# Three edits at the seam between attention and expert layers: hits in halves, two products on VectorE, a part of layer 1 moved

## The chip, the cores and the metric

The kernel runs on one core of a Trainium2 chip. The metric is the device time of one execution in microseconds; the median of three runs before the change is 376.25 us (375.22 to 376.61).

## The reference

The reference is two layers in a row. Attention without softmax: for each of 8 batches and 8 heads, a state kv of 64 by 64 is summed over 576 positions, each q row is multiplied by it, and the result is divided by its root mean square and multiplied by g_norm. The result is x, 4608 rows of 512. Then a layer of 8 experts with an early exit: a row whose skip score is not positive leaves as it is; every other row goes to the one expert with the greatest logit.

```python
kv = np.einsum('bhsd,bhse->bhde', k, v)
out = np.einsum('bhsd,bhde->bhse', q, kv)
rms = np.sqrt(np.mean(out * out, axis=-1, keepdims=True) + 1e-06)
x = out / rms * g_norm                       # then reshaped to 4608 x 512
do_compute = x @ w_skip > 0
e_idx = argmax(x @ w_gate);  gate_w = softmax probability of e_idx
out = x;  out[do_compute] += gate_w * (relu(x @ w1[e_idx]) @ w2[e_idx])
```

All inputs and the output are fp32; an expert's w1 is 512 x 1024, its w2 is 1024 x 512.

## The kernel before

The work has two stages, and the order of instructions on each engine is written out by hand.

**Attention.** 36 units (`units`, NU = 36) are stepped through by the loop `for n in range(NU + 2)`. A unit is four of the eight heads for about half of a batch's rows (the rows left over of four batches make units of their own): `turn` transposes q on TensorE, `values` multiplies by the state on TensorE into o_ps and squares on ScalarE (L514), `squares` reduces on VectorE (L522), `root` takes the root on ScalarE (L529), `norm` takes the reciprocal (L536) and multiplies on VectorE into `xl` (L545). On GpSimd `finish` adds the parts of the logits from `lp` to `lg` (L597 to L605), and `weigh` queues in `late` a product of x and g (`xb`, L615), which `scale` issues later. When both products of a pair of units are made, `store_x` writes 256 KB of x to the output by DMA, most of them on SP's queue (L639, L650). Jobs are put at named places of a step (`at(step, "early" | "mid" | "pe" | "dve" | "end", job)`): "mid" comes behind the step's `values` and ahead of its `squares` or `norm`.

**Choosing places.** The tokens are 36 tiles of 128. They come in three groups that end at tiles 12, 22 and 36. For each group `choose` finds the expert (up to `ohb`, L682), `rank` counts on TensorE into g_ps (L693 to L699), and `number` reads the ranks (`pr`, L710, and `top`, L711) and makes `hi_k` and the one-hot rows `oha_k` (L725) on VectorE. With the second group the order of the experts is known, and so are the columns of the 22 tiles up to there, the known tiles (NE = 22). `hits` (L739) compares their `hi_k` with the columns' names, `weighed` (L747) multiplies the hits by the rows' numbers into `bv`, and `place` (L759) sums on TensorE `oha_k` times `bv` into g_ps, over the columns where the ranks stood. The tags "ohc" and "bv" have one buffer each in `gat_pool`.

**The seam.** The last two units are treated apart: their logits come first (`last_logits`, L567 and L573), ScalarE multiplies them (`norm_by_scalar`, L582), and then, at step NU: `choose(LAST)`, all of `late` but one product on GpSimd behind it, `weighed` for the known tiles, `rank(LAST)`, `number(LAST)`, and the last product on GpSimd behind the last `oha_k`. Meanwhile TensorE runs a part of layer 1 of the first expert for 192 rows that were gathered early (`first_layer_1`, L856). After the attention pools are closed: `place` of the known tiles, `columns` of the other 14 tiles (hits and `bv`), two more columns of layer 1 (`first_1`, L1173, each of 128 hidden units), half of `layer_2` (L1185), `place` of the 14 tiles, the sum into `srow` (L817), the rest of the tables (L1112 to L1130, L823, L826), and the gathers of rows from the output in DRAM (L1145, on POOL's queue). The gathers read rows that the stores of x wrote, so they wait for these to land.

**Experts.** Eight experts in order of their load, with seven-product multiplications (`fast_1`, `fast_2`, L1253), the weights of the next loaded meanwhile; the results go out by indirect DMA (L1384, L1407).

Of the kernel before, what the change touches and what calls it, by code (L numbers as in the profile page):

```python
# [9 lines left out]
BF16 = mybir.dt.bfloat16  # L10
I32 = mybir.dt.int32
AX = mybir.AxisListType
ALU = mybir.AluOpType
# [4 lines left out]
def kernel(  # L18
# [43 lines left out]
    nc = tc.nc  # L62
# [3 lines left out]
    P = 128  # L66
# [5 lines left out]
    NT = NF * FQ * 2  # L72
# [14 lines left out]
    NCOL = E * CK  # L87
# [5 lines left out]
    keep = ctx.enter_context(tc.tile_pool(name="keep", bufs=1))  # L93
    wpool_a = ctx.enter_context(tc.tile_pool(name="wpool_a", bufs=1))
    gat_pool = ctx.enter_context(tc.tile_pool(name="gat", bufs=1))
# [52 lines left out]
    room = wpool_a.tile([P, FC, DM], FP32, tag="w2", name="w2")  # L148
    room = room[:, :, :].rearrange("p c d -> p (c d)")
# [25 lines left out]
    row128_i = keep.tile([P, P], I32)  # L175
# [29 lines left out]
    for i in range(KVD):  # L205
        t = kvd_pool.tile([P, 2, 2, 2, PK], FP32, name=f"kvd{i}")
# [25 lines left out]
    for a in range(2):  # L232
        r = slice(a * 64, (a + 1) * 64)
        nc.vector.tensor_scalar(out=gw_b[r, :, a, :, :],
                                in0=wraw[r, :, :].rearrange("e n (u w) -> e u w n", u=2),
# [28 lines left out]
    for i, qs in enumerate((slice(0, 4 * NQ), slice(4 * NQ, FQ))):  # L264
# [5 lines left out]
                                   op=ALU.bitwise_and)  # L270
    row_k = keep.tile([P, NT, 2], BF16)
    nc.vector.tensor_copy(out=row_k[:, :, 1], in_=rest_i[:, :, :, :].rearrange("p f t r -> p (f t r)"))
    nc.vector.tensor_tensor(out=row_k[:, :, 0], in0=row_i[:, :, :, :].rearrange("p f t r -> p (f t r)"),
                            in1=rest_i[:, :, :, :].rearrange("p f t r -> p (f t r)"), op=ALU.subtract)
# [4 lines left out]
    for r, cap in enumerate(ROOMS):  # L279
        pieces, off = [], 0  # L280
# [13 lines left out]
    for lo, m, _ in runs:  # L294

        if m < P and (lo, m) not in again:
            t = keep.tile([P, P], FP32, name=f"again{lo}_{m}")
# [3 lines left out]
        if m not in part_of:  # L301
# [5 lines left out]
                                           op=ALU.add)  # L307
# [5 lines left out]
    oha_k = keep.tile([P, NT, P], BF16)  # L313
# [7 lines left out]
        out=srow[:, :].rearrange("p (r c) -> p r c", c=CK),  # L321
        in0=beyond[:, :].unsqueeze(1).to_broadcast([P, E, CK]),
        in1=caps[:, :].unsqueeze(2).to_broadcast([P, E, CK]), op=ALU.is_ge)
# [104 lines left out]
    NU = len(units)  # L428
# [9 lines left out]
    late = []  # L438
# [3 lines left out]
    def at(step, part, job):  # L442
        todo.setdefault((step, part), []).append(job)
# [37 lines left out]
        half = slice(r * 64, (r + 1) * 64)  # L481
        return lambda: nc.scalar.copy(out=q8s[f][half, u, :, hf, :], in_=ps[half, :, 2 * PK:2 * PK + P])

    valued, counted = [], []

    def values(n):
        _, b, i, u = units[n]
# [121 lines left out]
    def weigh(n, xl):  # L609

        nq, b, i, u = units[n]
        if u == 0:
            xbs[nq] = xb_pool.tile([P, 2, DM], FP32, tag="xb", name="xb")
        xb = xbs[nq]
        late.append((lambda: nc.gpsimd.tensor_tensor(  # L615
            out=xb[:, :, 4 * u * D:(4 * u + 4) * D].rearrange("p r (w x) -> p r w x", w=2),
            in0=xl[:, :, :, G:G + 2 * D] if i is None else
            xl[:, :, :, G:G + 2 * D].rearrange("p w r x -> p r w x"),
            in1=g_b[:, :, :].rearrange("p a d -> p (a d)").unsqueeze(1).unsqueeze(1)
                .to_broadcast([P, 2, 2, 2 * D]), op=ALU.mult), u == 1 and (lambda: store_x(nq, b, i))))  # L620
    def scale(n, behind=None, keep=0):

        while len(late) > keep:
            job, store = late.pop(0)
            ins = job()
            if behind:
                tc.add_manual_dep(ins.ins, behind.ins.name, WAIT, reason="VectorE's port is free then")
            store = store() if store else None
            if store:
                at(min(n + 2, NU + 1), "end", store)  # L630
# [23 lines left out]
    ohbs, rks, chosen = {}, {}, []  # L654
# [49 lines left out]
    def number(g):  # L704

        t0, t1 = ([0] + ends)[g], ends[g]
        nt = t1 - t0
        ohb, rk = ohbs.pop(g), rks.pop(g)
        pr = gat_pool.tile([P, TG, E], FP32, tag="pr", name="pr")[:, 0:nt, :]
        nc.vector.tensor_tensor(out=pr, in0=rk[:, 0:nt, :], in1=ohb, op=ALU.mult)  # L710
        nc.vector.tensor_copy(out=top[:, :], in_=rk[:, nt, :])  # L711
        yield
        s_i = gat_pool.tile([P, TG], I32, tag="s_i", name="s_i")[:, 0:nt]
        with nc.allow_low_precision(reason="whole numbers"):
            nc.vector.tensor_reduce(out=s_i, in_=pr, axis=AX.X, op=ALU.add)
        yield
        lo_i = gat_pool.tile([P, TG], I32, tag="lo_i", name="lo_i")[:, 0:nt]
        nc.vector.tensor_single_scalar(out=lo_i, in_=s_i, scalar=127, op=ALU.bitwise_and)
        yield
        nc.vector.tensor_single_scalar(out=hi_k[:, t0:t1], in_=s_i, scalar=7,  # L720
                                       op=ALU.arith_shift_right)
        yield
        step = 2 if g < LAST else nt // 2
        for t in range(0, nt, step):
            counted.append(nc.vector.tensor_tensor(  # L725
                out=oha_k[:, t0 + t:t0 + t + step, :],
                in0=row128_i[:, :].unsqueeze(1).to_broadcast([P, step, P]),
                in1=lo_i[:, t:t + step].unsqueeze(2).to_broadcast([P, step, P]),
                op=ALU.is_equal))
            yield  # L730

    def drain(pieces):
        for _ in pieces:
            pass

    def hits(t0, nt, colid, pool, room):

        ohc = pool.tile([P, room, NCOL], BF16, tag="ohc", name="ohc")[:, 0:nt, :]
        nc.vector.tensor_tensor(  # L739
            out=ohc, in0=colid[:, :].unsqueeze(1).to_broadcast([P, nt, NCOL]),  # L740
            in1=hi_k[:, t0:t0 + nt].unsqueeze(2).to_broadcast([P, nt, NCOL]), op=ALU.is_equal)
        return ohc

    def weighed(ohc, t0, nt, val, pieces, pool, room):

        bv = pool.tile([P, room, pieces, NCOL], BF16, tag="bv", name="bv")[:, 0:nt, :, :]
        nc.vector.tensor_tensor(  # L747
            out=bv, in0=ohc.unsqueeze(2).to_broadcast([P, nt, pieces, NCOL]),
            in1=val[:, t0:t0 + nt, :].unsqueeze(3).to_broadcast([P, nt, pieces, NCOL]),
            op=ALU.mult)  # L750
        return bv

    def columns(t0, nt, colid, val, pieces, pool, room):
        return weighed(hits(t0, nt, colid, pool, room), t0, nt, val, pieces, pool, room)

    def place(ps, bv, t0, nt, first=True, last=True):

        for t in range(nt):
            nc.tensor.matmul(out=ps, lhsT=oha_k[:, t0 + t, :],  # L759
                             rhs=bv[:, t, :, :].rearrange("p i c -> p (i c)"),  # L760
                             start=(first and t == 0), stop=(last and t == nt - 1))

    colid_i = keep.tile([P, NCOL], I32)
# [70 lines left out]
    IN = 4  # L834
# [55 lines left out]
    NE = ends[LAST - 1]  # L890
    known_at = []
# [52 lines left out]
    for b in range(KNOWN // S // 4 * 4, KNOWN // S):  # L944
        nc.gpsimd.dma_start(
            out=out[b * S:(b + 1) * S, :].rearrange("(p c) d -> p c d", c=C)[:, C - 1, :],
# [19 lines left out]
    for b, n in starts.items():  # L966
        if b:
            step, counts = portions[b]
# [31 lines left out]
    for part in range(2):  # L1000
        at(NU - 3 + part, "pe", lambda part=part: first_in(part))
    at(NU - 1, "early", lambda: first_layer_1(range(1), slice(0, P)))
    at(NU - 1, "mid", lambda: known_at.append(hits(0, NE, colid_i, gat_pool, NE)))
    at(NU - 1, "end", first_rest)

    PACE = (2, 4)
    for n in range(NU + 2):
        now[0] = n
        if 1 <= n < NU - 1:
            turn(n + 1)  # L1010
        if 1 <= n <= NU:
            root(n - 1)
        jobs(n, "early")
        if n < NU:
            values(n)
        jobs(n, "mid")
        if THIRD + 2 <= n < NU:
            squares(n)
        done = norm(n - 1) if 1 <= n <= NU else None
        if n < THIRD + 2:  # L1020
            squares(n)
        jobs(n, "pe")
        if done:
            done()
        if n == NU:
            for pair, job in enumerate(last_x):
                job()
                first_hidden(pair)
            drain(choose(LAST))
            scale(NU, chosen[-1], 1)  # L1030
            first_bv = weighed(known_at[0], 0, NE, row_k, 2, gat_pool, NE)
            rank(LAST)
            drain(number(LAST))
            scale(NU, counted[-1])
        jobs(n, "dve")

        if n in ends[:LAST]:
            streams.append((PACE[ends.index(n)], gating(ends.index(n))))
        for pace, stream in streams:
            for job in itertools.islice(stream, pace):  # L1040
                if job:
                    part, job = job if isinstance(job, tuple) else ("pe", job)
                    at(n + 1, part, job)
                    break
        jobs(n, "end")
# [6 lines left out]
    with tc.tile_pool(name="wpool_b", bufs=1, reuse_waits="tile") as wpool_b, \  # L1052
# [477 lines left out]
        def first_1(fs):  # L1530
            layer_1(0, xt_first, ht0, slice(0, KEPT), fs)

        sp = g_ps[:, GB:GB + 2 * NCOL]
        place(sp, first_bv, 0, NE, True, False)
        last_bv = columns(NE, NT - NE, colid_i, row_k, 2, gat_pool, NE)
        first_1(range(IN, 6))
        y = layer_2(0, ht_of, first[0], None, range(IN))
        place(sp, last_bv, NE, NT - NE, False, True)
        add_pieces(srow[:, :], sp, 2)
        y_more = layer_2(0, ht_of, first[1], None, range(IN))  # L1540
        arows = gat_pool.tile([P, NRES], I32, tag="arows", name="arows")
# [35 lines left out]
        colid = slot_pool.tile([P, NCOL], I32)  # L1577
# [51 lines left out]
```

## Time and profile before

| | |
|---|---|
| median of 3 runs | 376.25 us |
| profiled execution's own time | 376.26 us |
| its span, first to last instruction | 374.4 us |
| TensorE busy | 363.2 us (97%) |
| VectorE busy | 244.3 us (65%) |
| ScalarE busy | 146.0 us (39%) |
| GpSimd busy | 123.1 us (33%) |
| mean granted TensorE clock | 0.996 |

In the profile PE is TensorE's multiplication and PEld its weight load, DVE is VectorE, ACT ScalarE, POOL GpSimd, and SP the engine whose queue issues most transfers. A row of a timeline has the start and the length in us, the engine, the line, the operation with its output and inputs, the number of instructions in it, and in brackets the idle time before it with what ended it. Matmuls overlap and their ends are modelled. A fp32 multiplication shows as two records.

### The profile page before, as it was taken

The page shows a single profiled execution, that of the slowest core. Times are in us where ns is not written, and L with a number is a line of the kernel's source. Part 1 is how long each engine was busy: PE and PEld are TensorE (multiplying, and loading weights), DVE is VectorE, ACT ScalarE, POOL GpSimd, SP SyncE. Part 2 cuts the span into 40 slices and gives each one's busy share as a digit, 9 for nine tenths or more (in the row PEclk, how much of TensorE's full clock was granted, in tenths as well). Part 3 has the DMA queues.
Part 4 walks back from the last instruction along what each step waited for, and adds up shares of the span by engine and source line. Part 5 has one row for each costly group of instructions (what it writes and reads, how often), then busy time and mean ns, then how long its engine had stood idle before and what let it go on. Part 6 is the DMA issues. An engine that isn't in the chain of part 4 may idle for free.

```text
span 374.4 us, 9661 instructions
## 1 busy us (share of the span) xinstructions
PE 363.2 (97%) x3859; PEld 315.2 (84%) x3859; DVE 244.3 (65%) x627; ACT 146.0 (39%) x398; POOL 123.1 (33%) x191
## 2 busy tenths in 40 slices
PE   8999999999999999999999999999999999999994
PEld 4687797898979679779879987988998998998983
DVE  2354458667878845676766675876876876878831
ACT  2366676676776222214403421430440440441420
POOL 7035457655768555223012303203202302102003
PEclk9999999999999999999999999999999999999998
DMA  7999999996499449966518263672762761700001
GB/s 290 393 391 391 401 403 394 404 384 201 130 330 311 111 109 325 395 204 226 203 53 268 69 226 103 225 254 54 259 228 47 273 230 61 269 3 32 26 1 53
DMA packets 32039, 81.70 MB, mean 218 GB/s; under 512 B 2474, under 2 KB 2482, under 8 KB 31988
## 3 DMA queue, kind: packets, MB, share of 16 engines
q1 hardware_dynamic: 28176, 69.47, 52.3%
q0 software_dynamic: 3792, 11.53, 9.2%
q8 instruction: 32, 0.52, 0.6%
q14 instruction: 19, 0.16, 0.1%
q10 hardware_dynamic: 20, 0.02, 0.0%
HBM read 66.80 MB, written 14.48 MB: 217 GB/s over the span
## 4 chain that ended last, share of the span: by engine, by line
PE 83%; issue 6%; POOL 4%; DVE 3%; ACT 3%; POOLq 0%; DVEq 0%; ACTq 0%
PE bank L1253 44%; PE bank L1185 9%; PE o_ps L498 7%; PE sum_ps L379 5%; PE bank L1173 4%; PE q_ps L460 3%; PE g_ps L393 2%; PE q_ps L170 2%; PE bank L1154 2%; POOL xb L615 2%; DVE xl L545 1%; DVE rs L522 1%; PE g_ps L411 1%; ACT qT L463 1%; ACT sq L514 1%
## 5 line engine op out<-in xcount | busy, mean ns | idle before, releaser
L1263 ACT COPY p<-bank 128x128 f32<-128x128 f32 (+6 forms) x70 | 20.8, 297 | 99.5 <-PE bank L1253 88.2
L1253 PE MATMUL bank<-xt,w 128*128 128x128 f32 (+5 forms) x336 | 55.5, 288 | 0.0
L615 POOL TENSOR_TENSOR xb<-xl,g_b 128x512 f32<-128x512 f32 x36 | 43.7, 1216 | 34.3 <-DVE rs L536 30.4
L1384 POOL DMA_INDIRECT out_dram<-xg,rows x14 | 14.0, 999 | 118.6 <-DVE xg L1381 115.4
L1253 PEld LDWEIGHTS bank<-xt,w 128*128 128x128 f32 x336 | 47.0, 190 | 1.9 <-DVE bank L1257 1.4
L1257 DVE TENSOR_TENSOR bank<-bank,p 128x128 f32<-128x128 f32 (+6 forms) x70 | 23.6, 338 | 30.2 <-PE bank L1253 29.0
L498 PE MATMUL o_ps<-kvd,qT 128*128 128x146 f32 x240 | 35.8, 290 | 1.0 <-ACT kvd L415 0.7
L1253 PE MATMUL bank<-xs,s 128*128 128x128 f32 (+5 forms) x224 | 36.7, 289 | 0.0
L522 DVE TENSOR_REDUCE rs<-sq 128x8 f32<-128x512 f32 x36 | 24.6, 682 | 15.6 <-ACT sq L514 15.5
L498 PEld LDWEIGHTS o_ps<-kvd,qT 128*128 128x128 f32 x240 | 31.6, 188 | 2.0 <-ACT kvd L415 1.5
L1253 PEld LDWEIGHTS bank<-xs,s 128*128 128x128 f32 x224 | 31.1, 190 | 1.0 <-ACT p L1263 0.8
L1185 PE MATMUL bank<-w,ht 128*32 128x128 f32 (+2 forms) x424 | 29.9, 313 | 0.0
L545 DVE TENSOR_TENSOR xl<-o_ps,rs 128x584 f32<-128x584 f32 x32 | 24.5, 767 | 4.3 <-DVE rs L536 0.5
L1185 PEld LDWEIGHTS bank<-w,ht 128*32 128x32 f32 (+2 forms) x424 | 18.2, 119 | 10.7 <-issue 7.6
L1253 PE MATMUL bank<-t,ht 128*128 128x256 f32 x112 | 27.0, 384 | 0.0
L1145 POOL DMA_INDIRECT xg<-out_dram,src x14 | 15.6, 1116 | 33.3 <-DMA out_dram<-xg,rows 18.0
L1253 PE MATMUL bank<-w,ht 128*128 128x256 f32 x112 | 26.5, 380 | 0.0
L514 ACT ACTIVATE sq<-o_ps 128x512 f32<-128x512 f32 x34 | 20.3, 597 | 15.0 <-PE o_ps L498 14.4
L379 PE MATMUL sum_ps<-v,k 64*64 64x64 f32 x1152 | 25.3, 227 | 0.4 <-issue 0.4
L1253 PE MATMUL bank<-t,hs 128*128 128x256 f32 x112 | 25.3, 379 | 0.0
L379 PEld LDWEIGHTS sum_ps<-v,k 64*64 64x64 f32 x1152 | 21.4, 138 | 4.5 <-issue 2.2
L1253 PEld LDWEIGHTS bank<-t,ht 128*128 128x128 f32 x112 | 20.8, 190 | 3.9 <-issue 1.2
(223 smaller groups left out, 679.2 us busy)
## 6 DMA issues: line engine op xcount, KB each, us to landing
w<-in_moe_w_dram SPq DMA_DIRECT2D x16, 2048.0 KB, 8.9
k<-in_k_dram SPq DMA_DIRECT2D x16, 576.0 KB, 9.9
v<-in_v_dram SPq DMA_DIRECT2D x16, 576.0 KB, 10.7
q<-in_q_dram SPq DMA_DIRECT2D x16, 576.0 KB, 10.2
out_dram<-xb SPq DMA_DIRECT2D x29, 256.0 KB, 9.8
out_dram<-xb POOLq DMA_DIRECT2D x7, 256.0 KB, 6.6
xg<-out_dram,src POOLq DMA_INDIRECT x16, 3.6
out_dram<-xg,rows POOLq DMA_INDIRECT x16, 6.2
```

What stands on the lines that cost most here:

```text
L379: nc.tensor.matmul(out=sum_ps[w * 64:(w + 1) * 64, a, u, :], lhsT=kt[r, 2 * u + w, c, :], rhs=vt[r, 2 * u + w, c, :], start=(c == 0), stop ...
L498: mm = nc.tensor.matmul(out=ps[:, w, 0:2 * PK].rearrange("p (r k) -> p r k", r=2)[:, :, cols], lhsT=qT[:, w, a, :], rhs=kvds[b % KVD][:, u ...
L514: nc.scalar.activation(out=sq[:, :, :, :], in_=heads(ps, G, G + 2 * D), func=ACT.Square)
L522: nc.vector.tensor_reduce(out=rs[:, :, :], in_=sq[:, :, :, :].rearrange("p x y (a d) -> p x (y a) d", a=2), axis=AX.X, op=ALU.add)
L545: nc.vector.tensor_tensor(out=xl[:, :, :, :].rearrange("p x y (a k) -> p x (y a) k", a=2), in0=ps[:, :, 0:2 * PK].rearrange("p x (h k) -> ...
L615: late.append((lambda: nc.gpsimd.tensor_tensor(out=xb[:, :, 4 * u * D:(4 * u + 4) * D].rearrange("p r (w x) -> p r w x", w=2), in0=xl[:, : ...
L1145: nc.gpsimd.indirect_dma_start(out=x_of(xg, off, m), out_offset=None, in_=cut_rows(m)[:, :], in_offset=bass.IndirectOffsetOnAxis(ap=idx[:, ...
L1173: nc.tensor.matmul(out=hps[:, cols], lhsT=w_sb[r][0][:, dc, f * P:(f + 1) * P], rhs=xt[:, dc, cols], start=(dc == 0), stop=(dc == DC - 1))
L1185: nc.tensor.matmul(out=yps[q * m:(q + 1) * m, 0:n], lhsT=ht(f)[:, off:off + m], rhs=w_sb[r][1][:, f, q * n:(q + 1) * n], start=(f == 0), s ...
L1253: nc.tensor.matmul(out=out, lhsT=lhsT(i), rhs=rhs(i), start=start and i == 0, stop=i == k - 1, skip_group_check=True)
L1257: nc.vector.tensor_tensor(out=to, in0=x, in1=y, op=ALU.add)
L1263: nc.scalar.copy(out=t, in_=x)
```

## The change

Three edits. The hits of the known tiles were one instruction over 22 tiles at step NU - 1; they become two over 11 tiles, at steps NU - 5 and NU - 3. Of the three products of x and g that were left to GpSimd at the end, two are now issued on VectorE, behind the hits and `bv` of the last 14 tiles, which are moved ahead of them out of the next stage; the wait of the last product on the last `oha_k` goes with that. And of the two columns of layer 1 behind the known tiles' placing, one (index 4) is issued ahead of it. Line numbers behind the last edits are 3 greater (L1173 becomes L1176, L1145 becomes L1148).

```diff
-        late.append((lambda: nc.gpsimd.tensor_tensor(
+        late.append((lambda eng: eng.tensor_tensor(
...
-    def scale(n, behind=None, keep=0):
+    def scale(n, behind=None, keep=0, eng=None):
...
-            ins = job()
+            ins = job(eng or nc.gpsimd)
...
-    def hits(t0, nt, colid, pool, room):
-
-        ohc = pool.tile([P, room, NCOL], BF16, tag="ohc", name="ohc")[:, 0:nt, :]
+    def hits(t0, nt, colid, pool, room, known=()):
+
+        all = known[0] if known else pool.tile([P, room, NCOL], BF16, tag="ohc", name="ohc")
+        ohc = all[:, t0:t0 + nt, :] if known else all[:, 0:nt, :]
...
-        return ohc
+        return all if room == NE else ohc
...
-        return weighed(hits(t0, nt, colid, pool, room), t0, nt, val, pieces, pool, room)
+        return weighed(hits(t0, nt, colid, pool, room)[:, 0:nt, :], t0, nt, val, pieces, pool, room)
...
-    at(NU - 1, "mid", lambda: known_at.append(hits(0, NE, colid_i, gat_pool, NE)))
+    for part in range(2):
+        at(NU - 5 + 2 * part, "mid", lambda part=part: known_at.append(
+            hits(part * NE // 2, NE // 2, colid_i, gat_pool, NE, known_at)))
...
-            scale(NU, chosen[-1], 1)
-            first_bv = weighed(known_at[0], 0, NE, row_k, 2, gat_pool, NE)
+            scale(NU, chosen[-1], 2)
+            first_bv = weighed(known_at[0][:, :, :], 0, NE, row_k, 2, gat_pool, NE)
             rank(LAST)
             drain(number(LAST))
-            scale(NU, counted[-1])
+            last_bv.append(columns(NE, NT - NE, colid_i, row_k, 2, gat_pool, NE))
+            scale(NU, eng=nc.vector)
...
+        first_1(range(IN, 5))
         place(sp, first_bv, 0, NE, True, False)
-        last_bv = columns(NE, NT - NE, colid_i, row_k, 2, gat_pool, NE)
-        first_1(range(IN, 6))
+        first_1(range(5, 6))
         y = layer_2(0, ht_of, first[0], None, range(IN))
-        place(sp, last_bv, NE, NT - NE, False, True)
+        place(sp, last_bv[0], NE, NT - NE, False, True)
```

## The prediction

> **What bounds the kernel now.** I read the page's busy times first, then who TensorE waits for, then the timelines of the engines around the change (100 to 150 us), and last the DMA issues there. Page, part 1:
>
> ```profile
> PE 363.2 (97%) x3859; PEld 315.2 (84%) x3859; DVE 244.3 (65%) x627; ACT 146.0 (39%) x398; POOL 123.1 (33%) x191
> ```
>
> TensorE leaves only 11.2 us of the 374.4 us span. Its waits from 123 us to 351 us (total, times, longest) are one line:
>
> ```profile
> PE g_ps L759 <- DVE top L711: 0.8, 1, 0.8
> ```
>
> So after 123 us the end moves one for one with TensorE, and one wait is left to take away. TensorE's timeline shows where it lies (start, us, line, operation):
>
> ```profile
> 119.18 2.76 PE L856 MATMUL q_ps<-xt_first,w 128*128 128x192 f32 x16
> 121.79 0.48 PE L693 MATMUL g_ps<-top,ident 128*128 128x120 f32 x2
> ...
> 122.33 0.59 PE L699 MATMUL g_ps<-ohb,ones 128*128 128x112 bf16 x14
> 123.71 0.71 PE L759 MATMUL g_ps<-bv,oha_k 128*128 128x48 bf16 x22 [0.79 <-DVE top L711]
> 124.27 2.85 PE L1173 MATMUL bank<-xt_first,w 128*128 128x192 f32 x16
> 126.95 3.60 PE L1185 MATMUL bank<-w,xg 128*128 128x512 f32 x8
> 130.38 0.51 PE L759 MATMUL g_ps<-bv,oha_k 128*128 128x48 bf16 x14
> ```
>
> The ranks end at 122.92, the placing of the known tiles starts at 123.71: 0.79 us idle. The placing overwrites the ranks' place in g_ps, so it waits until `pr` and `top` have been read out. VectorE's timeline:
>
> ```profile
> 117.66 0.71 DVE L739 TENSOR_TENSOR ohc<-colid_i,hi_k 128x528 bf16<-128x528 int32 x1
> ...
> 121.96 0.27 DVE L682 TENSOR_TENSOR ohb<-eorder,fi 128x112 bf16<-128x112 f32 x1
> 122.15 1.25 DVE L747 TENSOR_TENSOR bv<-ohc,row_k 128x1056 bf16<-128x1056 bf16 x1
> ...
> 123.50 0.15 DVE L711 COPY top<-g_ps 128x8 f32<-128x8 f32 x1
> ...
> 124.51 3.03 DVE L725 TENSOR_TENSOR oha_k<-row_i,lo_i 128x896 bf16<-128x896 int32 x2
> 127.46 0.50 DVE L739 TENSOR_TENSOR ohc<-colid_i,hi_k 128x336 bf16<-128x336 int32 x1
> 128.06 1.65 DVE L747 TENSOR_TENSOR bv<-ohc,row_k 128x672 bf16<-128x672 bf16 x1
> ```
>
> and GpSimd's:
>
> ```profile
> 117.77 0.72 POOL L597 TENSOR_TENSOR lp<-xl 128x36 f32<-128x36 f32 x1
> ...
> 120.26 0.22 POOL L605 TENSOR_TENSOR lg<-lp 128x18 f32<-128x18 f32 x1
> 122.31 3.28 POOL L615 TENSOR_TENSOR xb<-xl,g_b 128x512 f32<-128x512 f32 x2 [1.83 <-DVE ohb L682]
> 127.68 1.31 POOL L615 TENSOR_TENSOR xb<-xl,g_b 128x512 f32<-128x512 f32 x1 [2.10 <-DVE oha_k L725]
> ```
>
> To be seen: where both work from SBUF they hold each other up. The small `lp` sum takes 0.72 beside the hits at 117.66 and 0.25 elsewhere; of the two `oha_k` of 896 the first took 2.03 beside a product, the second, by the group's mean of 1.554, 1.08.
>
> **What the Trainium skill says.** "SBUF — State Buffer", section "Who interferes with whom": a VectorE instruction with two SBUF inputs contends with a GpSimd one that reads SBUF; the loser waits out the whole instruction. The rows above agree. "VectorE: DVE Perf Modes", section "The TRN2 errata": an fp32 tensor_tensor of N takes (N+151)/0.96 ns. The trace agrees: 691 ns worked out for 512 against 684 to 688 measured on L1195 and L1201. [...]the last stores of x, 256 KB each, take 3.2 us to landing here.
>
> **The change part by part.**
>
> Known tiles' hits in halves. The 0.71 us at 117.66 goes. Two of 264 come, (264+151)/0.96 = 0.43 us each (the same formula gives 0.71 for 528). By the order of instructions the first follows the second `src` of L912, which ends at 110.19; the next reduction starts at 110.73, idle 0.54 before it: the half fits, cost nothing. GpSimd's indirect load at 110.46 may start up to 0.15 later; its data land 2.9 us after issue, at 113.4, and TensorE turns them at 114.94. The second half follows the `xl` that ends at 114.12; the next reduction began at 114.45 after 0.33 idle, so it is pushed by 0.1. Behind it wait root, reciprocal and the `xl` of 115.38, which frees the o_ps bank for TensorE's 116.21. TensorE's loads pause 0.13 there already, so I charge 0 to 0.15, taken as 0.09. Without the cover of those idle places both halves would cost 0.86. At 117.66 GpSimd's `lp` drops from 0.72 to 0.25. GpSimd runs without a break there, so `lg` comes 0.47 earlier (120.0), and the choice, which waited for it at 120.51, ends near 121.77 instead of 122.23. That alone is worth nothing on TensorE: L856 fills it to 121.9, and ranks that take `ohb` begin at 122.28.
>
> A part of layer 1 between ranks and placing. L1173 is 2.85 us for 16 records; half of them, one f, is 1.43 us. It moves from behind the placing to ahead of it: TensorE's work is unchanged. Its inputs (xt_first, the first expert's w1) have been used since 115 us, and its instruction carries no wait in the changed order; the relu's ScalarE is free from 123.76. It runs 122.92 to 124.35. `bv` (122.95) and `top` (about 123.35, behind the ranks' end) are ready then, and would be even at today's 123.40 and 123.65. Gain 0.79. If nothing were put there, the earlier choice could give at most about 0.3, since `pr` must still wait for the ranks.
>
> Last two products on VectorE. GpSimd keeps one product behind the choice (about 121.85 to 124.0). Gone: the second, 124.40 to 125.59, and the third, 127.68 to 128.99. VectorE loses 2.03-1.08 = 0.95 on the first `oha_k`, and the last `bv` comes from 1.65 to 0.84 (by the slope from 1056 in 1.25 to 1296 in 1.51). Its chain: `lo_i` still shares the port to 124.0, `oha_k` twice 124.1 to 126.25, hits 0.50, `bv` 126.75 to 127.6. The `bv` buffer is single, so it waits for the known tiles' placing, now ending at 124.35+0.71 = 125.06: no wait. Then two products at 0.685 each (nearest row: L1195, same size and type; bounds 0.6 and GpSimd's 1.31) to 128.95. GpSimd's ended at 128.99, so SP's two stores at L639 keep their place. Behind them on VectorE waits the sum into srow, which needs the second placing (129.6 to 130.15): already free. TensorE reaches that placing 0.75 earlier, at 129.65, with data ready at 127.6 (before: 129.71 against 130.38).
>
> Then the tables, the gathers of L1145 (on POOL's queue, the first at 134.46 released by VectorE's `src`) and everything behind them move with TensorE. Stores land at 128.95+0.03+0.68+3.2 = 132.9, `src` comes at 134.23-0.75 = 133.5, so the stores are not what the gathers wait for.
>
> Sum: -0.79 +0.09 = -0.70 us. Span 374.4 to 373.7; the profiled execution's own 376.26, with 1.86 outside the span, to 375.56; the median of 376.25 is the same within 0.01, so I say 375.5. The runs of before spread from 375.22 to 376.61, twice what I forecast.
>
> **The rivals.**
>
> Eaten on the attention side. The second half pushes a chain that reaches TensorE, and the halves may meet GpSimd's loads. For: the chain of waits passes DVE L545 and L522 here. Against: 0.54 and 0.33 of idle time against 0.43 each. Fully exposed it is +0.86-0.79, so 376.3; half of it 375.9.
>
> Slower: the last stores come late. The mechanism is VectorE's own queue: products stand behind `bv` and ahead of srow, and the gathers wait for the landed stores. With the products' end at t, stores land at t+3.9. Gathers are late from t = 129.6. The second gather, issued at 135.81, lands 3.0 later at 138.8, TensorE's load of it comes at 139.4: 0.6 to spare, so TensorE stalls from t = 130.2, the gain is gone at 130.9, and 0.5% is lost at 132.8. Were `oha_k` and `bv` not quickened (+0.95, +0.81) and products took 1.31 each (+1.25), t is 131.96: 376.26+1.06 = 377.3. Against: GpSimd has nothing to do then but a 0.18 us memset.
>
> More than I count. If removing 0.47 on GpSimd also lets TensorE start the end of attention earlier, its other idle time from 106 to 116 us (0.37+0.31+0.05) is the limit: -0.79-0.4 gives 375.1. Against: that lies ahead of the hits that go.
>
> The change does nothing, as the place is still late: needs `top` later than 124.35, 0.7 us later than now. 376.25.
>
> **How the numbers follow.** Forecast as worked out 0.63, with the spread of a median 374.9 to 376.1; eaten in part or whole 0.13; more 0.07; late stores 0.12; nothing happens 0.05. The range takes in the forecast, the eaten gain, the greater gain and the lower end of the late stores, and leaves out the rest, under two in ten: 374.6 to 376.9. About 0.5%, 1.9 us, is what a measurement of this kernel can tell from no change. Faster by that needs 374.37, more than twice my sum and beyond the idle time there is: 0.06. Slower by that, above 378.1, takes late stores whose stall also holds the gathers behind, somewhat over half of that case: 0.07. Same 0.87.
>
> **What would show it.** Right: TensorE has no wait at the known tiles' placing, an L1176 group of half size ahead of it at about 122.9, the last `oha_k` pair at 2.2 us, last `bv` under 0.9, products at 0.69 on VectorE ending near 129.0, the first gather near 133.7. Wrong: a TensorE wait at L1157 or at the second placing, a gather released by a DMA, a wait of o_ps L508 for VectorE over 0.2, or a new wait after 140 us, where I take the rest to move unchanged.

## The result and the profile after

The changed kernel takes 374.74 us against 376.12 us for the kernel before, medians of 22 runs each. The ratio is 0.9967 (0.9958 to 0.9976), a gain of 1.24 us with an interval from 0.90 to 1.58. The two medians themselves differ by 1.38: the run times of each kernel fall into two clusters (last section), and a median that lies near the gap between them jumps easily. The forecast was 375.5, a gain of 0.70 within a range of 374.6 to 376.9. So the time lies in the range, 0.14 us above its lower end, and within 0.5% of no change, but the gain is almost twice the sum.

The profiled execution took 374.1 us with a span of 372.2, which is 2.2 us less than the span before. Only half of that is the change. The start of the kernel, where nothing was edited, differs by 1.07 us; the last section shows it. To leave it out, all that follows is counted from the start of the last L856 group on TensorE (119.18 before, 118.10 after), and on this count the end comes at 254.13 instead of 255.20.

The busy times after, from the page's first part:

```profile
PE 361.7 (97%) x3859; PEld 314.4 (84%) x3859; DVE 243.4 (65%) x630; ACT 145.9 (39%) x398; POOL 119.9 (32%) x189
```

TensorE now leaves 10.5 us of the span where it left 11.2. Its timeline after (start, us, line, operation):

```profile
118.10 2.76 PE L856 MATMUL q_ps<-xt_first,w 128*128 128x192 f32 x16
120.70 0.38 PE L693 MATMUL g_ps<-top,ident 128*128 128x120 f32 x2
120.92 0.21 PE L696 MATMUL g_ps<-ohb,ut 128*128 128x112 bf16 x1
...
121.42 1.55 PE L1176 MATMUL bank<-xt_first,w 128*128 128x192 f32 x8
122.80 0.72 PE L759 MATMUL g_ps<-bv,oha_k 128*128 128x48 bf16 x22
...
124.75 3.60 PE L1188 MATMUL bank<-w,xg 128*128 128x512 f32 x8
128.18 0.51 PE L759 MATMUL g_ps<-bv,oha_k 128*128 128x48 bf16 x14
```

The half group of layer 1 (L1176) stands between the ranks and the placing (L759), and the bracket with the 0.79 us wait for `top` is gone. From 121 to 351 us the view of TensorE's waits has no line left. Now compare L693 with the row shown before the change: 0.48 us for two instructions there, 0.38 here, with L696 0.49 and 0.22 us behind its start. This small difference turns out to be a quarter of the gain.

VectorE's and GpSimd's timelines after:

```profile
112.28 0.77 DVE L545 TENSOR_TENSOR xl<-o_ps,rs 128x584 f32<-128x584 f32 x1
112.96 0.42 DVE L739 TENSOR_TENSOR ohc<-colid_i,hi_k 128x264 bf16<-128x264 int32 x1
113.38 0.69 DVE L522 TENSOR_REDUCE rs<-sq 128x8 f32<-128x512 f32 x1
...
120.43 0.28 DVE L682 TENSOR_TENSOR ohb<-eorder,fi 128x112 bf16<-128x112 f32 x1
...
122.98 2.09 DVE L725 TENSOR_TENSOR oha_k<-row_i,lo_i 128x896 bf16<-128x896 int32 x2
...
125.60 0.86 DVE L747 TENSOR_TENSOR bv<-ohc,row_k 128x672 bf16<-128x672 bf16 x1
126.38 1.29 DVE L615 TENSOR_TENSOR xb<-xl,g_b 128x512 f32<-128x512 f32 x2
```

```profile
116.71 0.25 POOL L597 TENSOR_TENSOR lp<-xl 128x36 f32<-128x36 f32 x1
...
120.78 2.13 POOL L615 TENSOR_TENSOR xb<-xl,g_b 128x512 f32<-128x512 f32 x1 [1.83 <-DVE ohb L682]
...
132.74 1.05 POOL L1148 DMA_INDIRECT xg<-out_dram,asrc  x1 [9.67 <-ACT ht L1178]
```

The durations are close to the forecast: half of the hits 0.42, `lp` 0.25 instead of 0.72, the last `oha_k` pair 2.09 instead of 3.03, the last `bv` 0.86 instead of 1.65, two products in 1.29 (forecast 1.37). The `lp`, `oha_k` and `bv` rows agree with the Trainium skill, "SBUF — State Buffer", section "Who interferes with whom": each was long while the other engine also worked from SBUF, and is short now that it doesn't.

### The profile page after: what moved, and what is told of

The parts are those of the page before. It is cut to its first block, busy times and chain, and to the rows that moved or that the text cites. A ratio compares the mean times of both kernels' runs of the same rounds, so it can differ in the third digit from the quotient of the medians.

```text
span 372.2 us, 9661 instructions
## 1 busy us (share of the span) xinstructions
PE 361.7 (97%) x3859; PEld 314.4 (84%) x3859; DVE 243.4 (65%) x630; ACT 145.9 (39%) x398; POOL 119.9 (32%) x189
## 4 chain that ended last, share of the span: by engine, by line
PE 87%; issue 5%; ACT 3%; POOL 2%; DVE 1%; POOLq 0%; ACTq 0%; DVEq 0%
PE bank L1256 45%; PE bank L1188 9%; PE o_ps L498 7%; PE sum_ps L379 5%; PE q_ps L460 4%; PE bank L1176 4%; PE g_ps L393 2%; PE q_ps L170 2%; PE bank L1157 2%; PE g_ps L856 1%; PE g_ps L411 1%; ACT qT L463 1%; PE o_ps L508 1%; PE q_ps L856 1%; PE g_ps L402 1%
## 5 line engine op out<-in xcount | busy, mean ns | idle before, releaser
L615 POOL TENSOR_TENSOR xb<-xl,g_b 128x512 f32<-128x512 f32 x34 | 41.3, 1216 | 32.1 <-DVE rs L536 30.3
L498 PE MATMUL o_ps<-kvd,qT 128*128 128x146 f32 x240 | 35.8, 290 | 1.0 <-ACT kvd L415 0.7
L522 DVE TENSOR_REDUCE rs<-sq 128x8 f32<-128x512 f32 x36 | 24.6, 682 | 14.5 <-ACT sq L514 14.4
L498 PEld LDWEIGHTS o_ps<-kvd,qT 128*128 128x128 f32 x240 | 31.5, 188 | 2.0 <-ACT kvd L415 1.5
L1148 POOL DMA_INDIRECT xg<-out_dram,src x14 | 15.3, 1092 | 33.0 <-DMA out_dram<-xg,rows 17.3
L379 PE MATMUL sum_ps<-v,k 64*64 64x64 f32 x1152 | 24.7, 223 | 0.4 <-issue 0.4
L379 PEld LDWEIGHTS sum_ps<-v,k 64*64 64x64 f32 x1152 | 20.9, 134 | 4.3 <-issue 1.8
```

Of the source, the lines that this page charges most:

```text
L379: nc.tensor.matmul(out=sum_ps[w * 64:(w + 1) * 64, a, u, :], lhsT=kt[r, 2 * u + w, c, :], rhs=vt[r, 2 * u + w, c, :], start=(c == 0), stop ...
L498: mm = nc.tensor.matmul(out=ps[:, w, 0:2 * PK].rearrange("p (r k) -> p r k", r=2)[:, :, cols], lhsT=qT[:, w, a, :], rhs=kvds[b % KVD][:, u ...
L522: nc.vector.tensor_reduce(out=rs[:, :, :], in_=sq[:, :, :, :].rearrange("p x y (a d) -> p x (y a) d", a=2), axis=AX.X, op=ALU.add)
L615: late.append((lambda eng: eng.tensor_tensor(out=xb[:, :, 4 * u * D:(4 * u + 4) * D].rearrange("p r (w x) -> p r w x", w=2), in0=xl[:, :, ...
L1148: nc.gpsimd.indirect_dma_start(out=x_of(xg, off, m), out_offset=None, in_=cut_rows(m)[:, :], in_offset=bass.IndirectOffsetOnAxis(ap=idx[:, ...
```

## The experiments

The theory taken over from the prediction is that the layer-1 column alone gives the time by closing the 0.79 us gap, and that the halves give TensorE nothing. The shorter L693 suggests another theory, which the expectations below call "my theory": the halves give a part too, because an earlier choice (`ohb`) takes away a wait that L693's record hides. The other rivals: the products give a part; or the gain comes from the attention stage. A further question is whether the gathers wait for the stores. Single edits and complements of them separate these. The table has the start of each event in us, counted from the start of the last L856 group in the same trace.

| kernel | `ohb` ends | L696 starts | known tiles' placing | layer 2 starts | last `bv` ends | second placing | first gather | TensorE loads gathered rows |
|---|---|---|---|---|---|---|---|---|
| before | 3.05 | 3.10 | 4.53 | 7.77 | 10.53 | 11.20 | 15.28 | 20.61 |
| layer_only | 3.07 | 3.12 | 5.00 | 6.94 | 10.56 | 10.61 | 14.91 | 20.02 |
| halves_only | 2.59 | 2.82 | 4.07 | 7.30 | 10.07 | 10.74 | 14.81 | 20.15 |
| products_only | 3.07 | 3.12 | 4.55 | 7.79 | 8.82 | 11.22 | 15.30 | 20.64 |
| no_layer | 2.58 | 2.81 | 4.05 | 7.29 | 8.32 | 10.72 | 14.80 | 20.14 |
| no_halves | 3.05 | 3.10 | 4.98 | 6.93 | 8.93 | 10.36 | 15.21 | 19.77 |
| no_products | 2.59 | 2.82 | 4.70 | 6.64 | 10.08 | 10.13 | 14.44 | 19.54 |
| after | 2.61 | 2.82 | 4.70 | 6.65 | 8.36 | 10.08 | 14.64 | 19.49 |
| products_first | 2.59 | 2.82 | 4.70 | 6.64 | 9.54 | 10.08 | 14.15 | 19.49 |
| late_1 | 2.60 | 2.82 | 4.70 | 6.64 | 8.47 | 10.07 | 16.20 | 19.59, then a stall |

The last column is where TensorE first needs what the gathers bring, so it is the time that counts here; the last section compares what follows it. The first four experiments ran on one chip, where the kernel before took 377.09 us (59 runs); the other four on another, where it took 375.74 (53 runs). Each ratio is to the kernel before on its own chip.

**layer_only.** The kernel before with the layer-1 column moved and nothing else:

```diff
+        first_1(range(IN, 5))
         place(sp, first_bv, 0, NE, True, False)
         last_bv = columns(NE, NT - NE, colid_i, row_k, 2, gat_pool, NE)
-        first_1(range(IN, 6))
+        first_1(range(5, 6))
```

> The kernel before, with nothing but the part of layer 1 moved between ranks and placing. The stage is measured from the start of the last L856 group to the start of the first L1185 group: 7.77 us before, 6.65 after. My theory: the move closes the 0.79 us wait at the known tiles' placing and nothing else, the ranks still begin with a hidden wait of about 0.27 for ohb: stage 6.98, time -0.8 us. The second placing may wait 0.1, since its bv is not earlier. Rival A (the whole gain comes from freeing the port by the products): the wait only moves on to the second placing, stage above 7.4, time within 0.3 of before. Rival B (what lies beyond 0.79 is only the start-up of the profiled execution): this kernel already has the whole gain, -1.2 us, stage 6.65.

Measured: 376.15 us, ratio 0.9981 (0.9972 to 0.9990). TensorE's timeline:

```profile
121.97 0.48 PE L693 MATMUL g_ps<-top,ident 128*128 128x120 f32 x2
122.46 0.21 PE L696 MATMUL g_ps<-ohb,ut 128*128 128x112 bf16 x1
...
126.28 3.60 PE L1185 MATMUL bank<-w,xg 128*128 128x512 f32 x8
129.95 0.51 PE L759 MATMUL g_ps<-bv,oha_k 128*128 128x48 bf16 x14
```

Layer 2 starts 0.83 us earlier (7.77 to 6.94): the gap is closed as forecast. But the second placing comes only 0.59 earlier. It starts 3.67 us behind the layer-2 group here, against 3.43 in the kernels before and after: it waits 0.24 for the last `bv`, which ends at 10.56, and no bracket shows that wait, because the length printed for the layer-2 group is the same 3.60 in both. So the column alone is worth 0.59, and the rest needs an earlier last `bv`. L693 still has its 0.48. Neither rival of the expectation holds: layer 2 starts at 6.94, neither above 7.4 nor at 6.65.

**halves_only.** The kernel before with the hits in two halves and nothing else:

```diff
...
-    at(NU - 1, "mid", lambda: known_at.append(hits(0, NE, colid_i, gat_pool, NE)))
+    for part in range(2):
+        at(NU - 5 + 2 * part, "mid", lambda part=part: known_at.append(
+            hits(part * NE // 2, NE // 2, colid_i, gat_pool, NE, known_at)))
...
```

The parts left out are those of `hits` and its callers, as in the whole change.

> The kernel before with nothing but the known tiles' hits in two halves. My theory: GpSimd's lg and so ohb come 0.46 us earlier; the ranks lose a hidden wait of 0.27, bv and top end 0.46 earlier, and so does the placing: stage 7.3, time -0.45 us. Rival A: 0, stage 7.77. The prediction as it was written: at most -0.3, and the halves themselves cost up to 0.1 on TensorE.

Measured: 376.79 us, ratio 0.9985 (0.9975 to 0.9995). TensorE's timeline:

```profile
121.67 0.38 PE L693 MATMUL g_ps<-top,ident 128*128 128x120 f32 x2
121.89 0.21 PE L696 MATMUL g_ps<-ohb,ut 128*128 128x112 bf16 x1
...
123.14 0.71 PE L760 MATMUL g_ps<-bv,oha_k 128*128 128x48 bf16 x22 [0.60 <-DVE top L711]
```

The gathered rows are loaded 0.46 us earlier. That comes in two pieces. The ranks start 0.28 earlier (3.10 to 2.82), with L693 at 0.38. And the gap ahead of the placing is 0.60 instead of 0.79, because the known tiles' `bv` ends earlier and `top` is read out 0.56 us behind the ranks' end instead of 0.73. The step that gave the earlier choice no value on TensorE falls here.

**products_only.** The changed kernel with the hits whole again and both columns behind the placing:

```diff
-    for part in range(2):
-        at(NU - 5 + 2 * part, "mid", lambda part=part: known_at.append(
-            hits(part * NE // 2, NE // 2, colid_i, gat_pool, NE, known_at)))
+    at(NU - 1, "mid", lambda: known_at.append(hits(0, NE, colid_i, gat_pool, NE)))
...
-        first_1(range(IN, 5))
         place(sp, first_bv, 0, NE, True, False)
-        first_1(range(5, 6))
+        first_1(range(IN, 6))
```

> The kernel before with nothing but the last columns and the last two products on VectorE. My theory: nothing on TensorE waits for them in the kernel before, stage 7.77, time 0.0 (within 0.2); the last bv ends 1.8 us earlier. Rival A (the products are what pays): -0.4 us or more, stage below 7.4.

Measured: 376.94 us, ratio 1.0005 (0.9995 to 1.0016). TensorE's row at the placing, then VectorE's last `bv`:

```profile
122.92 0.71 PE L759 MATMUL g_ps<-bv,oha_k 128*128 128x48 bf16 x22 [0.79 <-DVE top L711]
```

```profile
126.33 0.86 DVE L747 TENSOR_TENSOR bv<-ohc,row_k 128x672 bf16<-128x672 bf16 x1
```

The last `bv` has its short form and ends 1.71 us earlier (8.82 against 10.53), and TensorE gains nothing: the gap of 0.79 is untouched, and the second placing was never late for this `bv`. Alone, the products give slack only.

**no_layer.** The changed kernel with both columns of layer 1 behind the placing, as before:

```diff
-        first_1(range(IN, 5))
         place(sp, first_bv, 0, NE, True, False)
-        first_1(range(5, 6))
+        first_1(range(IN, 6))
```

> The changed kernel without the moved part of layer 1: halves and products alone. My theory: as with the halves alone, stage 7.3, time -0.45 us, with a wait of about 0.6 at the known tiles' placing. Rival A: -0.8 us or more. Rival B: 0 to -0.2 us.

Measured: 376.06 us, ratio 0.9981 (0.9968 to 0.9993). Its stages are those of halves_only to 0.02 us in all of TensorE's columns, though its last `bv` comes 1.75 earlier; the gap ahead of the known tiles' placing is the same 0.60. The time alone, whose interval spans gains of 0.3 to 1.2 us, doesn't tell this from rival A; the columns do.

So without the column the products add nothing to the halves, and the column is worth 0.65 us in the changed kernel (20.14 to 19.49).

**no_halves.** The changed kernel with the hits whole at step NU - 1:

```diff
-    for part in range(2):
-        at(NU - 5 + 2 * part, "mid", lambda part=part: known_at.append(
-            hits(part * NE // 2, NE // 2, colid_i, gat_pool, NE, known_at)))
+    at(NU - 1, "mid", lambda: known_at.append(hits(0, NE, colid_i, gat_pool, NE)))
```

> The changed kernel with the hits of the known tiles in one piece at their old place: layer 1 and products alone. Measured from the start of the last L856 group (second placing: 11.20 us before, 10.08 in the changed kernel, 10.61 with the move of layer 1 alone). My theory: the ranks' hidden wait of 0.28 is back, the second placing has its bv early, so it comes at 10.36 to 10.4, time -0.8 us against before. A rival in which the products give time of their own: below 10.2.

Measured: 374.76 us, ratio 0.9976 (0.9965 to 0.9986). TensorE's timeline:

```profile
120.52 0.48 PE L693 MATMUL g_ps<-top,ident 128*128 128x120 f32 x2
121.01 0.21 PE L696 MATMUL g_ps<-ohb,ut 128*128 128x112 bf16 x1
```

The 0.48 of L693 is back, and everything behind it is 0.28 us later than in the changed kernel: ranks 3.10 against 2.82, placing 4.98 against 4.70, second placing 10.36 against 10.08, load of the gathered rows 19.77 against 19.49. Against layer_only the second placing is 0.25 earlier: here the short last `bv` pays.

**no_products.** The changed kernel with two products on GpSimd again, the last of them behind the last `oha_k`:

```diff
...
-            scale(NU, chosen[-1], 2)
+            scale(NU, chosen[-1], 1)
...
+            scale(NU, counted[-1])
             last_bv.append(columns(NE, NT - NE, colid_i, row_k, 2, gat_pool, NE))
-            scale(NU, eng=nc.vector)
```

`counted` collects the `oha_k` instructions, as in the kernel before.

> The changed kernel with the last two products back on GpSimd behind the choice and behind the last oha_k, the last columns where they are in the changed kernel: halves and layer 1 alone. My theory: nothing is lost up to the first L1188 group (6.65), then the last bv ends at 10.07 as with the halves alone, just where TensorE wants it: second placing at 10.1 to 10.2, time -1.0 to -1.1 us. The rival (the products carry a part of the gain): second placing 10.4 or later, time -0.8 us or less.

Measured: 374.73 us, ratio 0.9974 (0.9961 to 0.9988). VectorE's row:

```profile
126.18 1.65 DVE L748 TENSOR_TENSOR bv<-ohc,row_k 128x672 bf16<-128x672 bf16 x1
```

This `bv` ends at 10.08, and the placing that needs it could start at 10.08. It starts at 10.13, so with the other two edits in place the products are worth 0.05 us.

**products_first.** The changed kernel with the two products ahead of the last hits and `bv` on VectorE, so that the stores go out earlier:

```diff
+            scale(NU, eng=nc.vector)
             last_bv.append(columns(NE, NT - NE, colid_i, row_k, 2, gat_pool, NE))
-            scale(NU, eng=nc.vector)
```

> The changed kernel with the two products ahead of the last columns on VectorE. My theory: stores and the first gather are bound by the products in the changed kernel (first gather 14.64, 0.48 later than its table allows); here the products end 1.36 earlier, the first gather comes at 14.2, the last bv ends at 9.65, still ahead of 10.08. No time on TensorE: second placing 10.08, load of the gathered rows 19.49, time as the changed kernel, -1.1 to -1.2 us. If gathers are bound by something else, the gather stays at 14.64.

Measured: 375.05 us, ratio 0.9974 (0.9962 to 0.9985), the same as the changed kernel. GpSimd's queue:

```profile
133.24 1.05 POOL L1148 DMA_INDIRECT xg<-out_dram,asrc  x1 [9.21 <-DVE src L826]
```

The products end 1.40 us earlier (8.16 against 9.56), and the first gather goes out 0.49 us earlier, at 14.15 instead of 14.64, though the first part of the tables that name its rows (`asrc`) is made at the same place, 13.29 and 13.30. Here it starts 0.23 us behind the end of `src`; in the changed kernel it starts 0.72 behind. In the changed kernel, then, the gather does wait for the stores. TensorE doesn't notice either way (19.49 in both).

**late_1.** The changed kernel with each of the two products issued twice on VectorE (the second issue writes the same values again), which delays the stores:

```diff
+            for _ in range(1 if eng else 0):
+                job(eng)
             ins = job(eng or nc.gpsimd)
```

> The changed kernel with each of the two VectorE products issued twice (the same output again), which ends them 1.29 us later. The prediction's rival of late stores, with its price: stores and first gather 1.29 later (15.9), the gathered rows have only about 0.1 us to spare, so TensorE's load of them stalls, 20.6 to 20.7 instead of 19.49; time about that of the kernel before (-0.1 to +0.2 us). If the stores are hidden anyway: 19.49 and -1.1 us.

Measured: 375.48 us, ratio 0.9992 (0.9980 to 1.0003). GpSimd and TensorE:

```profile
135.29 1.05 POOL L1150 DMA_INDIRECT xg<-out_dram,asrc  x1 [11.27 <-DVE colid L1583]
```

```profile
139.67 0.33 PE L1159 MATMUL bank<-ident,xg 128*128 128x128 f32 x1 [0.34 <-DMA xg<-out_dram,asrc]
```

The products end 1.56 us later (11.12 against 9.56), and the first gather is later by just that, 16.20 against 14.64. In both kernels it goes out 5.08 us behind the products' end. TensorE waits for a gather in the bracket of L1159, 0.34 us. The whole loss is more: the layer-2 group behind these loads starts 20.84 us after the last L856 group, against 20.13 in the changed kernel, 0.71 later. So of 1.56 us about 0.85 was spare. On this chip products_first keeps a gain of 0.26%; with the stores this late 0.08% is left. Both the delay and the price were only roughly foreseen. The two more products add 1.45 us instead of 1.29, and another 0.11 comes from ahead of them: `lo_i` takes 0.67 us in this trace and 0.55 in the changed kernel's, and no_halves, where nothing is doubled, has 0.67 too. And the stall was smaller than expected, since not 0.1 but 0.85 us was spare.

## Why the prediction was right or wrong

**The gap at the known tiles' placing: right.** The forecast was 0.79 from moving one column. layer_only moves the start of layer 2 by 0.83. The half group stands between the ranks and the placing, as forecast, and the placing has no wait.

**"That alone is worth nothing on TensorE": wrong, and the largest miss.** The earlier choice was costed at nothing because L856 seemed to fill TensorE up to the ranks: L693 ended at 122.27 and the ranks began at 122.28. But L693's own record held the wait. Its two instructions show 0.48 where a choice at 3.05 or 3.07 ends late and 0.38 where it ends by 2.61. In all four kernels of the first kind (before, layer_only, products_only, no_halves) L696 starts 0.05 behind `ohb`; in all six of the second it starts at 2.81 or 2.82, 0.2 behind it. The step should have said: TensorE can reach L696 0.28 us sooner, and this wait ends with `ohb`. The term is -0.28 instead of 0 with the column in place. The prediction's side remark that the earlier choice "could give at most about 0.3" without the column missed the same piece: halves_only gave 0.46, of which 0.19 is the shrunken gap the remark meant.

**The second half's push, +0.09: not there.** From the last L498 group on sum_ps to the last L856 group TensorE took 6.73 us before and 6.72 after. VectorE's rows before, at the place of the second half:

```profile
113.35 0.77 DVE L545 TENSOR_TENSOR xl<-o_ps,rs 128x584 f32<-128x584 f32 x1
114.45 0.69 DVE L522 TENSOR_REDUCE rs<-sq 128x8 f32<-128x512 f32 x1 [0.33 <-ACT sq L514]
```

The idle time of 0.33 was thought to be too short for 0.43. Yet after the change the hits start at 112.96, before the end printed for the `xl` ahead of them (112.28 + 0.77 = 113.05), so neighbouring records overlap by 0.09, and 0.33 + 0.09 holds the 0.42. The reduction starts 1.10 us behind the start of that `xl` both before and after, so there is no push. The first half costs nothing either: the traces are 1.07 us apart on TensorE at 34 us, ahead of both halves, and 1.08 at the last L856 group. That the attention side takes or gives nothing also settles two rivals, "eaten on the attention side" and "more than I count".

**The sum.** -0.79 + 0.09 = -0.70 was forecast; -0.83 and -0.28 and nothing give -1.11, and the traces show -1.12 in each TensorE column from the start of layer 2 on (20.61 to 19.49 in the last). The measured gain of 1.24 (0.90 to 1.58) agrees with this and not with 0.70. That the time still fell into the range is in part luck: its lower end had been set for the rival "more than I count", and that rival's mechanism is not what gave the gain.

**The products: right in kind.** No time by themselves (products_only 1.0005), and each of their durations as forecast. What the working did not say is where the slack is needed: with the column moved and the hits whole, a long last `bv` would have cost 0.25 us at the second placing; with the halves it costs 0.05. They insure the other two edits.

**"So the stores are not what the gathers wait for": wrong for the changed kernel.** For the kernel before, the step's reading holds:

```profile
134.46 1.05 POOL L1145 DMA_INDIRECT xg<-out_dram,asrc  x1 [5.34 <-DVE src L826]
```

The gather starts 0.23 us behind the end of `src` there, and so it does in halves_only, products_only, no_layer and products_first. In the other five kernels it starts later than that, and always 5.07 or 5.08 us behind the end of the last product, whether VectorE makes that product or GpSimd. The prediction let the gather go as soon as the stores had landed, 3.9 us behind the products' end; the term is 5.08. In the changed kernel the second store is issued at 128.37 and lands 3.2 us later, at about 131.6; the gather goes out at 132.74, some 1.2 us behind that. That the stores decide is shown by both sides: 1.40 earlier moves the gather by 0.49, until the tables hold it, and 1.56 later by 1.56. The row after the change names ScalarE's `ht` instead, which ended 0.02 us ahead of the gather; in products_first the gather goes out at 133.24, before that `ht` has started (133.38). What fills the 1.2 us on GpSimd's queue, no run separates. That the gather came at 14.64, near the forecast 133.7 (14.5 on this count), is luck: the tables were ready earlier than forecast and the stores held it back. The mistake cost no time, since about 0.85 us was spare where the prediction had estimated 0.6.

**The rival with late stores: its mechanism exists, and the change stays short of it.** It put the point from which gathers are late at products' end 129.6 in the clock of the kernel before, and TensorE's stall at 130.2. With 119.18 as that clock's zero, the runs put the first at 14.15 - 5.08 = 9.07, or 128.25, and the second at 9.56 + 0.85 = 10.41, or 129.6. Of the stall's 0.6, about 0.4 is the extra gain of TensorE itself. The products ended at 9.56, inside the margin. The 0.5% loss of that rival was not tried.

## What to carry to other kernels

Before an earlier operand is costed at nothing because the engine shows no wait, compare the length of the record just ahead of the consumer, and the distance between starts, with those of the same group elsewhere: in a pipelined engine's trace a wait can sit inside the record before it. Two seams of this kernel hid 0.24 and 0.27 us in that way. An edit that only makes slack should be tried together with the edits that use it; alone it shows nothing, and its worth (here 0, 0.05 or 0.25 us) depends on what else has moved. And the releaser that a row names is only the last event seen, right in the kernel before here and wrong in the changed one: to learn whether a transfer is what counts, move the transfer alone, both ways.

## What was not expected of the hardware

**The start of an execution has two lengths.** TensorE's timeline of before and of after, where nothing was edited:

```profile
6.89 1.03 PE L170 MATMUL q_ps<-ones 128*128 128x512 bf16 x2
```

```profile
6.60 0.60 PE L170 MATMUL q_ps<-ones 128*128 128x512 bf16 x2
```

The same two multiplications take 1.03 us and 0.60, and the 72 small ones behind them (L379) take 1.88 and 1.28; from there both run alike, and 1.07 us remains to the seam. At the very start of either trace two such multiplications take 1.03 or 1.04 us, so in the kernel before the slow pace of the start lasted longer. Run times of either kernel cluster some 1.1 us apart (373.7 to 374.5 and 374.9 to 375.8 for the changed one), which fits an execution starting in one way or the other. The ten traces fit it too. In four of them (after, products_only, no_halves, no_products) the 72 take 1.28 us and the last L856 group starts at 117.75 to 118.37 us; in the other six they take 1.85 to 2.15 and it starts at 119.07 to 119.78. Each of the four profiled runs is among the four shortest of its kernel, and none of the six is. Why an execution starts in one way or the other stays open. For the reader it means that two profiled spans of this kernel can differ by nearly the whole gain for no reason in the code, so stages have to be compared from a mark behind the start.

**A stop that nothing explains.** In all four kernels of the first chip TensorE stops once for 0.35 to 0.53 us in the midst of a later placing, with no releaser but "issue"; layer_only's row is

```profile
147.13 0.36 PE L759 MATMUL g_ps<-bv,oha_k 128*128 128x72 bf16 x6 [0.53 <-issue]
```

No other trace has it there. The same four have a second wait that no other has, at about 244 us, where TensorE waits 0.29 to 0.77 us for VectorE. From the load of the gathered rows to the end these four traces take 235.4 to 235.9 us, and the others 234.5 to 234.6 (late_1, with its stall, 235.2). So the ends of these four traces can't be compared with the end of before; the table's columns, which lie ahead of both, can. The kernel before took 377.09 us on that chip, and 376.12 and 375.74 us in the other two comparisons; whether the stop and the second wait are a part of that difference was not tried, and no trace of the kernel before shows them. Both were in products_only as well as in the others, so they don't bear on which edit gives the time.
